# One backward-attention kernel: the dO columns evacuated and summed for four heads at a time instead of two

## The chip, the cores and the metric

The kernel runs on one core of one Trainium2 chip. The metric is the device time of one execution in microseconds (us), as a median over several runs.

## The reference

It computes the forward pass and all gradients of one decode step of a transformer block with conditioning: attention over a cached K and V (2 batches, 32 heads, 8192 positions, 128 wide, bf16), then a gated feed-forward network. Cut to what matters:

```python
q = (h @ wq) per head
scores = einsum('bhqd,bhkd->bhqk', q, k_cache) * Dh ** -0.5
p = softmax(scores); o = einsum('bhqk,bhkd->bhqd', p, v_cache)
x = x + ga * (o @ wo)
...                                   # feed-forward, then jax.vjp of everything
out = (forward, d_x, d_k_cache, d_v_cache, d_wq, d_wo, ...)
```

K and V are 134 MB each. K is read once, V twice (forward and backward), and dK and dV, 134 MB each, are written.

## The kernel before

The program lays all work into numbered slots; within a slot each engine gets its instructions in a fixed order. A head has a forward job A (scores, softmax, o) and a backward job C (dP = dO V, dS, then the outer products dK and dV). In the middle of the run A jobs of batch 1 alternate with C jobs of batch 0; in the last third only C jobs of batch 1 are left.

A C job needs, for its head, the column dO = wo d_attn, that column times the softmax's normaliser (DOr), and SIG, the sum over the width of O times dO. These are made for two heads at a time, in three steps of one slot each:

```python
def steps_do(b, k):
    st = {}
    hs = slice(2 * k, 2 * k + 2)

    def tr():          # 8 transposes of wo blocks, evacuated to kt (DVE in batch 0, ACT in batch 1)
        ...
    def mm():
        ps = scr(2)    # scratch columns in the PSUM tile that the head's scores or dP use as well
        kt = st.pop("kt")
        for n in range(2):
            for dc in range(NC):
                nc.tensor.matmul(ps[:, n:n + 1], kt[:, n * NC + dc, :], d_attn_bf[:, dc, b:b + 1], ...)
        nc.vector.tensor_copy(DO_bf[:, b, hs], ps)
        nc.vector.tensor_mul(DOr_bf[:, b, hs], ps, rtot[:, b, hs])
        pr = tmp.tile([P, 2], F32, name="prod", tag="prod", bufs=2)
        nc.vector.tensor_mul(pr[:], O32[:, b, hs], ps)
        st["pr"] = pr

    def sig():
        ps = scr(2)
        nc.tensor.matmul(ps, onesf[:], st.pop("pr")[:], start=True, stop=True)
        nc.vector.tensor_copy(SIG[:, b, hs], ps)

    return [(1, tr), (1, mm), (1, sig)]
```

`scr` hands out columns 256 and up of the tile `s_ps`, in whose columns 0 to 63 the dP matmuls of the running C job are written. Batch 0's pairs are spread over the run, each a few slots before its heads need it. Batch 1's 16 pairs come one after another, two slots apart, once d_attn of batch 1 is known:

```python
for k in range(H // 2):
    lay(steps_do(0, k), E0 if k == 0 else max(E0 + 3 * k, sC[2 * k] - 10))
...
for k in sorted(range(H // 2), key=lambda k: 2 * k < H - VKEEP):   # the two heads whose V is kept come first
    lay(steps_do(1, k), t1)
    t1 += 2
```

A finished half of dK or dV (1 MB) is stored from its tile, and that tile comes free for the next load only after the store has landed (in the kernel before, the median store landed 12.8 us after its issue; page, part 6):

```python
if o + QK == HK:
    sq_.dma_start(src_of(dst, n)[:, hf * HK:(hf + 1) * HK, :], t[:])   # 1 MB store
    ...                                                             # tile released 6 slots later
```

## Time and profile before

| what | value | view |
|---|---|---|
| time, median of 6 runs | 1748.55 us (1748.49 to 1749.08) | runs |
| span of the profiled run | 1745.8 us | page |
| DMA traffic | 713.55 MB, mean 409 GB/s | page, slices |
| PE, DVE, ACT busy | 79%, 67%, 57% | page, part 1 |
| batch 1's dO stretch | 69.5 us, clock 0.59 | windows |

Batch 1's **stretch** means here the time from the start of the DVE instruction that writes d_attn of batch 1 to the end of the last SIG copy: 1147.92 to 1217.44 us.

From the page of the kernel before: the rows of part 2 cut the span into 40 equal slices; a digit is a share in tenths.

```profile
span 1745.8 us, 54866 instructions
PE 1384.8 (79%) x24113; PEld 1236.8 (71%) x24113; DVE 1170.4 (67%) x1677; ACT 986.7 (57%) x1405; POOL 368.9 (21%) x646
...
PE   6999999989967777777776778788777776785783
...
PEclk9999999988988978888888888775655556566576
DMA  9999999999999999999999999999999999999997
GB/s 381 417 418 417 418 417 390 417 378 415 419 423 410 413 419 419 419 413 415 407 415 411 416 405 398 371 422 423 425 416 420 417 406 397 417 420 411 405 415 315
DMA packets 112955, 713.55 MB, mean 409 GB/s; under 512 B 11303, under 2 KB 20211, under 8 KB 30795
```

The DMA row is full in all slices but the last, and the rate is 405 to 425 GB/s in 33 of the 40 slices. PE is nearly full in the first quarter (412.95 of the first 440 us, by the windows view) and no engine is after that. I read that as a kernel bound by transfers; half_before, sum_x5 and keep0 below test it. The clock row is in tenths of full speed, so 9 is 90% or more and 5 is half.

The waits of the kernel before, whole run. Columns: who waited, for whom, us in total, times, the longest.

```profile
DVE half L1088 <- DMA out_dram<-half: 248.2, 75, 10.6
...
PE s_ps L1065 <- DVE prod L731: 14.2, 22, 1.3
DVE SIG L737 <- PE s_ps L736: 13.9, 16, 1.1
```

The same view of the load queue:

```profile
SPq L177 <- DMA out_dram<-half: 753.0, 92, 18.9
```

Both DVE's outer products (L1088) and the loads (L177) wait most for stores to land.

The windows of the kernel before. Each row: stretch, its length, then busy us (and instructions) of each engine, granted clock, DMA share (1.01 over 0 to 440 and 470 to 1000 us too, where the DMA row is at 9), GB/s.

```profile
core 0: us, PE busy (x) PEld busy (x) DVE busy (x) ACT busy (x) POOL busy (x), PEclk, DMA share, GB/s
1147.92:1217.44 69.52, 59.44 (x815) 56.67 (x813) 50.16 (x115) 41.84 (x53) 8.51 (x16) 0.59 1.01 422
1217.44:1240.00 22.56, 17.10 (x294) 14.95 (x293) 14.39 (x20) 14.81 (x22) 2.35 (x5) 0.76 1.01 425
```

One pair of heads, in order of time. Columns: start, duration, engine, line, operation, output and inputs; in brackets the idle time before it and who ended it.

```profile
1156.36 0.15 DVE L728 CAST DO_bf<-s_ps 128x2 bf16<-128x2 f32 x1
...
1156.49 0.15 DVE L731 TENSOR_TENSOR prod<-O_266,s_ps 128x2 f32<-128x2 f32 x1
...
1156.70 0.34 PE L1065 MATMUL s_ps<-DO_bf,kt 128*128 128x1 bf16 x8 [1.32 <-DVE prod L731]
...
1156.90 0.36 PE L736 MATMUL s_ps<-prod,onesf 128*128 128x2 f32 x2
...
1157.69 0.15 DVE L737 COPY SIG<-s_ps 128x2 f32<-128x2 f32 x1
```

The dP matmuls (L1065) do not use prod, but they write into the PSUM tile that prod still reads, and here PE sat idle for 1.32 us until prod was through. The whole run has 22 such waits, 14.2 us in all.

### The profile page before, as it was taken

The numbers are of one execution on the slowest core, as the hardware profiler recorded it, in microseconds if no ns is written. First come the engines' busy times: TensorE is split into PE (matmuls) and PEld (weight loads), VectorE is DVE, ScalarE is ACT, GpSimd is POOL, SyncE is SP. The second block draws the span as 40 slices with busy tenths as digits, with TensorE's granted clock in tenths as the row PEclk, the third lists the DMA queues.
The fourth block names the chain that finished last, engine by engine and source line by source line (L and its number), as shares of the span: only waits on it lengthen the run. The fifth ranks groups of instructions, "written<-read, shape, count | busy, mean of one in ns | idle before, by whom it ended". The sixth has DMA issues, their size and how long they took to land. (4 is left out here: it accounts for less than half of the span.)

```text
span 1745.8 us, 54866 instructions
## 1 busy us (share of the span) xinstructions
PE 1384.8 (79%) x24113; PEld 1236.8 (71%) x24113; DVE 1170.4 (67%) x1677; ACT 986.7 (57%) x1405; POOL 368.9 (21%) x646
## 2 busy tenths in 40 slices
PE   6999999989967777777776778788777776785783
PEld 5999999979866667677676677778555554574573
DVE  2666666857776676677667668777566666675686
ACT  4666666646544545555454455565656565574683
POOL 0333333312221221222122122111111111110111
PEclk9999999988988978888888888775655556566576
DMA  9999999999999999999999999999999999999997
GB/s 381 417 418 417 418 417 390 417 378 415 419 423 410 413 419 419 419 413 415 407 415 411 416 405 398 371 422 423 425 416 420 417 406 397 417 420 411 405 415 315
DMA packets 112955, 713.55 MB, mean 409 GB/s; under 512 B 11303, under 2 KB 20211, under 8 KB 30795
## 3 DMA queue, kind: packets, MB, share of 16 engines
q1 hardware_dynamic: 70832, 425.81, 60.2%
q0 software_dynamic: 36864, 268.45, 36.9%
q10 hardware_dynamic: 5019, 15.78, 2.3%
q8 instruction: 188, 3.08, 0.7%
q14 instruction: 52, 0.43, 0.1%
HBM read 425.79 MB, written 284.20 MB: 407 GB/s over the span
## 5 line engine op out<-in xcount | busy, mean ns | idle before, releaser
L371 ACT COPY kt<-tp 128x1024 bf16<-128x1024 bf16 x768 | 773.9, 1014 | 574.7 <-PE tp L366 566.4
L366 PE MATMUL tp<-identb,half 128*128 128x128 bf16 x8192 | 778.4, 252 | 13.5 <-DVE kt L369 11.1
L366 PEld LDWEIGHTS <-half 128*128 128x128 bf16 x8192 | 605.3, 113 | 102.8 <-issue 97.5
L1093 POOL DMA_DIRECT2D out_dram<-half x256 | 136.2, 532 | 1036.2 <-DVE half L1088 869.3
L427 PE MATMUL m_ps<-ek,half 128*128 128x129 bf16 x4096 | 325.2, 221 | 0.0
L369 DVE COPY kt<-tp 128x1024 bf16<-128x1024 bf16 x256 | 176.3, 688 | 167.9 <-PE tp L366 166.4
L1065 PE MATMUL s_ps<-DO_bf,kt 128*128 128x1 bf16 x4096 | 192.4, 168 | 114.0 <-DVE kt L369 93.3
L1065 PEld LDWEIGHTS <-kt 128*128 128x128 bf16 x4096 | 188.7, 108 | 129.9 <-DVE kt L369 103.8
L386 PE MATMUL s_ps<-qT_bf,kt 128*128 128x1 bf16 x4096 | 177.6, 164 | 102.6 <-DVE kt L369 100.8
L427 PEld LDWEIGHTS <-half 128*128 128x128 bf16 x4096 | 245.9, 98 | 0.3
L386 PEld LDWEIGHTS <-kt 128*128 128x128 bf16 x4096 | 158.9, 97 | 107.5 <-DVE kt L369 105.0
L1216 ACT CAST stg<-m_ps 128x512 bf16<-128x512 f32 (+2 forms) x124 | 72.2, 582 | 71.0 <-PE m_ps L1215 71.0
L449 PE MATMUL k_ps<-half,pz 128*32 128x512 bf16 x1024 | 68.0, 386 | 21.3 <-POOL pz L435 21.3
L1215 PE MATMUL m_ps<-half 2*128 2x512 bf16 (+2 forms) x124 | 74.1, 598 | 2.1 <-ACT half L1190 1.8
L449 PEld LDWEIGHTS <-pz 128*32 128x32 bf16 x1024 | 21.9, 96 | 41.6 <-POOL pz L435 23.4
L395 PE MATMUL s_ps<-nident,rm 128*128 128x128 bf16 x64 | 15.5, 243 | 22.0 <-DVE rm L390 22.0
L398 DVE TENSOR_REDUCE nm<-s_ps 128x1 f32<-128x128 f32 x64 | 18.6, 290 | 20.3 <-PE s_ps L395 20.3
L1298 ACT COPY kt<-tp 128x1024 bf16<-128x1024 bf16 x28 | 29.0, 1061 | 1.1 <-PE tp L1292 1.0
L712 PE MATMUL tp<-identb,half 128*128 128x128 bf16 x256 | 29.3, 287 | 0.0
L1190 ACT CAST half<-m_ps 2x512 bf16<-2x512 f32 (+1 forms) x36 | 19.9, 564 | 15.8 <-PE m_ps L1187 12.9
L712 PEld LDWEIGHTS <-half 128*128 128x128 bf16 x256 | 24.9, 139 | 0.0
L718 ACT COPY kt<-tp 128x1024 bf16<-128x1024 bf16 x16 | 16.2, 1012 | 14.0 <-PE tp L712 13.5
(871 smaller groups left out, 1766.5 us busy)
## 6 DMA issues: line engine op xcount, KB each, us to landing
out_dram<-half POOLq DMA_DIRECT2D x256, 1024.0 KB, 12.8
half<-in_A_v_cache_dram SPq DMA_DIRECT2D x252, 1024.0 KB, 11.7
half<-in_A_k_cache_dram SPq DMA_DIRECT2D x128, 1024.0 KB, 19.8
out_dram<-stg ACTq DMA_DIRECT2D x22, 512.0 KB, 9.9
half<-in_A_wq_dram SPq DMA_DIRECT2D x8, 1024.0 KB, 10.0
half<-in_B_w_dram SPq DMA_DIRECT2D x6, 1024.0 KB
half<-in_A_wo_dram SPq DMA_DIRECT2D x4, 1024.0 KB, 20.5
half<-in_w_mod_dram SPq DMA_DIRECT2D x3, 1024.0 KB, 16.6
```

Source lines behind the costliest of these rows:

```text
L366: nc.tensor.transpose(tp[:, j, :], block(j), identb[:])
L369: nc.vector.tensor_copy(kt[:], tp[:])
L371: nc.scalar.copy(kt[:], tp[:])
L386: nc.tensor.matmul(S_ps[i][:, cc:cc + 1], kt[:, j, :], qT_bf[:, h, b:b + 1], start=True, stop=True)
L427: nc.tensor.matmul(m[:, 0:P + 1], vb_(i, kk), t[:, kk % QK, 0:P + 1], start=(kk == 0), stop=(kk == KK - 1), skip_group_check=True)
L449: nc.tensor.matmul(kp["ps"][NR * j:NR * (j + 1), :], pz[:, o:o + NR], K[(i, kk // HK)][:, kk % HK:kk % HK + QP, :], start=False, stop=(h = ...
L712: nc.tensor.transpose(tp[:, n * NC + dc, :], wo_of(h, dc), identb[:])
L1065: nc.tensor.matmul(DP[n][:, cc:cc + 1], kt[:, j, :], DO_bf[:, b, h:h + 1], start=True, stop=True)
L1093: sq_.dma_start(src_of(dst, n)[:, hf * HK:(hf + 1) * HK, :], t[:])
L1215: nc.tensor.matmul(ps[:lw, 0:rw], rsl(ln, lc, lw, step), rsl(rn, rc, rw), start=True, stop=True)
L1216: nc.scalar.copy(st["t"][:lw, o:o + rw], ps[:lw, 0:rw])
L1298: nc.scalar.copy(kt[:], tp[:])
```

## The change

Its intent: do these small operations half as often. The transposes and the dO matmuls stay as they are, but two pairs share one scratch block, and one set of evacuations, one ones matmul and one SIG copy. The diff, cut:

```diff
-    def steps_do(b, k):
+    def steps_do(b, k0, k1):
...
-        hs = slice(2 * k, 2 * k + 2)
+        n2 = 2 * (k1 - k0)
+        hs = slice(2 * k0, 2 * k1)
-        def tr():
+        def tr(k):
...
-        def mm():
-            ps = scr(2)
+        def mm(k):
+            if k == k0:
+                st["ps"] = scr(n2)
+            ps = st["ps"]
             kt = st.pop("kt")
             for n in range(2):
+                o = 2 * (k - k0) + n
...                                        # matmuls into column o in place of n
+            if k < k1 - 1:
+                return
             nc.vector.tensor_copy(DO_bf[:, b, hs], ps)
             nc.vector.tensor_mul(DOr_bf[:, b, hs], ps, rtot[:, b, hs])
-            pr = tmp.tile([P, 2], F32, name="prod", tag="prod", bufs=2)
-            nc.vector.tensor_mul(pr[:], O32[:, b, hs], ps)
+            pr = tmp.tile([P, DOG * 2], F32, name="prod", tag="prod", bufs=2)
+            nc.vector.tensor_mul(pr[:, 0:n2], O32[:, b, hs], ps)
...
-        return [(1, tr), (1, mm), (1, sig)]
+        for k in range(k0, k1):
+            out += [(1, lambda k=k: tr(k)), (1, lambda k=k: mm(k))]
+        return out + [(1, sig)]
+
+    DOG = 2
...
-    for k in range(H // 2):
-        lay(steps_do(0, k), E0 if k == 0 else max(E0 + 3 * k, sC[2 * k] - 10))
+    for k in range(0, H // 2, DOG):
+        lay(steps_do(0, k, k + DOG), E0 if k == 0 else max(E0 + 3 * k, sC[2 * k] - 10))
...
-    for k in sorted(range(H // 2), key=lambda k: 2 * k < H - VKEEP):
-        lay(steps_do(1, k), t1)
-        t1 += 2
+    kf = (H - VKEEP) // 2
+    for k0, k1 in [(kf, H // 2), *((k, min(k + DOG, kf)) for k in range(0, kf, DOG))]:
+        lay(steps_do(1, k0, k1), t1)
+        t1 += 2 * (k1 - k0)
```

The number of slots that batch 1's stretch takes is the same.

More of the change, by code (lines that the diff above doesn't have):

```diff
@@ L719, in tr @@
             st["kt"] = kt
-        def mm():
-            ps = scr(2)
+        def mm(k):
+            if k == k0:
+                st["ps"] = scr(n2)
+            ps = st["ps"]
             kt = st.pop("kt")
             for n in range(2):
+                o = 2 * (k - k0) + n
                 for dc in range(NC):
-                    nc.tensor.matmul(ps[:, n:n + 1], kt[:, n * NC + dc, :], d_attn_bf[:, dc, b:b + 1],
+                    nc.tensor.matmul(ps[:, o:o + 1], kt[:, n * NC + dc, :], d_attn_bf[:, dc, b:b + 1],
                                      start=(dc == 0), stop=(dc == NC - 1))
+            if k < k1 - 1:
+                return
             nc.vector.tensor_copy(DO_bf[:, b, hs], ps)
             nc.vector.tensor_mul(DOr_bf[:, b, hs], ps, rtot[:, b, hs])
-            pr = tmp.tile([P, 2], F32, name="prod", tag="prod", bufs=2)
-            nc.vector.tensor_mul(pr[:], O32[:, b, hs], ps)
+            pr = tmp.tile([P, DOG * 2], F32, name="prod", tag="prod", bufs=2)
+            nc.vector.tensor_mul(pr[:, 0:n2], O32[:, b, hs], ps)
             st["pr"] = pr
         def sig():
-            ps = scr(2)
-            nc.tensor.matmul(ps, onesf[:], st.pop("pr")[:], start=True, stop=True)
+            ps = scr(n2)
+            nc.tensor.matmul(ps, onesf[:], st.pop("pr")[:, 0:n2], start=True, stop=True)
             nc.vector.tensor_copy(SIG[:, b, hs], ps)
-        return [(1, tr), (1, mm), (1, sig)]
+        for k in range(k0, k1):
+            out += [(1, lambda k=k: tr(k)), (1, lambda k=k: mm(k))]
+        return out + [(1, sig)]
+    DOG = 2
     def steps_chain(b):
```

## The prediction

> **What bounds the kernel now.** The DMA engines. The page's slices show DMA at 9 (90% or more) in 39 of 40 slices; 713.55 MB move at a mean of 409 GB/s in a span of 1745.8 us. The page's busy shares are lower: PE 79%, DVE 67%, ACT 57%. [...] In the waits of the load queue, loads wait 753.0 us for output stores to drain, by far the longest entry.
>
> **What the change does.** Batch 0's dO pairs are scattered from 448 to 1084 us. All 16 pairs of batch 1, and the last of batch 0, lie between 1146.1 and 1217.5 us. By the instruction order, transposes, their evacuations and the 256 d_attn matmuls stay; groups go from 32 to 17 (8 in batch 0, 9 in batch 1, where the kept pair stays alone and first). Each group has four small DVE operations (DO, DOr, prod, SIG) and one fp32 matmul against ones, recorded as two passes. So 60 DVE instructions of 0.15 to 0.16 us vanish, and 30 PE records of 0.22 to 0.35 us with weight loads of 0.19 to 0.34 us. The rest grow from 2 to 4 columns, which I take to cost nothing visible. No transfer is added, and the load queue's order stays.
>
> **Worth.** DVE: the timeline has three of the four starting 0.07 us apart, so a group takes about 0.4 us: 15 x 0.4 = 6 us, about half of it where batch 1's stretch leaves DVE idle anyway (52 of 71 us busy). PE: at most 15 x 0.6 = 9 us of records. Waits: PE's dP matmuls, whose PSUM tile holds the scratch columns, waited for prod 14.2 us (7.6 in batch 1's stretch); DVE waited 13.9 us for the ones matmul. About half of these should go. If engines bounded batch 1's stretch, it could shorten by 3 to 6 us of 71.
>
> **On the critical path: almost nothing.** In that stretch the windows view gives a DMA share of 1.01 and 423 GB/s, among the best of the run; loads mostly wait for stores (56.1 us), and 14 us for transposes. Engine time gained becomes longer waits for DMA. From 470 to 1000 us the share is 1.01 at 415 GB/s too. The new cost is latency: SIG and DOr of the first four heads come two slots (about 2.5 to 3 us) later, just before head 0's spread; loads in flight should hide it. Buffers freed a little earlier or later may shift the mix of reads and writes, a few us in either direction.
>
> **Prediction: 1748.0 us**, 8 in 10 between 1743.0 and 1752.0. Faster by over 2%: 0.01; within 2%: 0.98; slower by over 2%: 0.01.
>
> **What would show it right.** DO, DOr, prod and SIG at 17 each with unchanged means; DVE busy about 9 us lower by records (60 x 0.15), PE some 8 lower; PE's waits for prod about halved; DMA bytes unchanged, slices still 9; the load queue's waits for stores unchanged or longer; batch 1's stretch within 1 us of 71.4.
>
> **What would make it wrong.** If the stretch from 1146 us shortens by several us and the end moves with it, engines, not DMA, set the pace there. If the later DOr delays the first heads' stores enough to open a gap in DMA near 450 to 470 us, it gets slower. If the last 46 us (DMA share 0.77) change, the tail moved.

## The result, and the profile after

The changed kernel took 1748.24 us (median of 10 runs, 1744.65 to 1750.76), the kernel before 1748.87 us (20 runs, 1747.46 to 1752.12). The ratio is 0.9993, with a 95% interval of 0.9984 to 1.0001: the same.

The page of the changed kernel:

```profile
span 1746.7 us, 54749 instructions
PE 1366.7 (78%) x24083; PEld 1219.9 (70%) x24083; DVE 1165.6 (67%) x1617; ACT 987.1 (57%) x1405; POOL 372.8 (21%) x646
...
PEclk7999999989978888888888888787555556567576
DMA  9999999999999999999999999999999999999997
GB/s 381 417 418 418 418 417 388 418 378 418 419 422 404 412 422 418 413 417 419 415 411 411 407 412 399 381 418 422 427 414 420 419 399 394 416 416 408 405 413 319
DMA packets 112954, 713.54 MB, mean 408 GB/s; under 512 B 11303, under 2 KB 20211, under 8 KB 30795
```

Bytes and DMA row are as before. 60 DVE and 30 PE instructions are gone. But PE's busy time fell by 18.1 us, about twice what those 30 records can account for, and the clock row differs where the stretch lies (slices 27 and 28).

Its waits (L1076 is what L1065 was, L1099 what L1088 was, L737, L742 and L743 what L731, L736 and L737 were):

```profile
DVE half L1099 <- DMA out_dram<-half: 274.2, 75, 19.0
...
PE s_ps L1076 <- DVE prod L737: 2.3, 4, 0.8
...
DVE SIG L743 <- PE s_ps L742: 1.1, 1, 1.1
```

And its load queue:

```profile
SPq L177 <- DMA out_dram<-half: 792.2, 101, 16.8
```

The two waits that the change aims at went from 28.1 to 3.4 us. The waits for stores grew: by 26.0 us on DVE and by 39.2 us for the loads of L177 (27.4 us over all lines of the load queue). Part of that is scatter: in re_before below, the same kernel as before, DVE waited 257.7 us for stores in place of 248.2 and L177 763.9 in place of 753.0. The windows show where the time went:

```profile
core 0: us, PE busy (x) PEld busy (x) DVE busy (x) ACT busy (x) POOL busy (x), PEclk, DMA share, GB/s
1147.18:1201.89 54.71, 45.08 (x797) 42.83 (x795) 47.20 (x83) 41.47 (x53) 8.51 (x16) 0.80 1.01 423
1201.89:1240.00 38.11, 15.64 (x294) 13.88 (x293) 14.26 (x19) 14.41 (x22) 2.13 (x4) 0.65 1.01 424
```

The stretch is 14.8 us shorter (54.7 against 69.5), with the clock at 0.80 against 0.59. But the next row is 15.5 us longer with the same work in it (294 matmuls in both kernels), so by 1240 us the two kernels have done the same matmuls and are level again. The DVE timeline of the changed kernel shows the handover (the `...` stand for lines left out):

```profile
1212.28 1.22 DVE L1099 TENSOR_TENSOR half<-DOr,e_25217 128x2048 bf16<-128x2048 bf16 x1
1232.46 1.22 DVE L1099 TENSOR_TENSOR half<-Qr,ds_25441 128x2048 bf16<-128x2048 bf16 x1 [18.96 <-DMA out_dram<-half]
1237.42 1.23 DVE L1099 TENSOR_TENSOR half<-DOr,e_25533 128x2048 bf16<-128x2048 bf16 x1 [3.74 <-DMA out_dram<-half]
```

The same place in the kernel before:

```profile
1227.02 1.23 DVE L1088 TENSOR_TENSOR half<-Qr,ds_25531 128x2048 bf16<-128x2048 bf16 x1 [3.86 <-DMA out_dram<-half]
...
1232.16 1.22 DVE L1088 TENSOR_TENSOR half<-Qr,ds_25531 128x2048 bf16<-128x2048 bf16 x1
1237.12 1.23 DVE L1088 TENSOR_TENSOR half<-DOr,e_25623 128x2048 bf16<-128x2048 bf16 x1 [3.74 <-DMA out_dram<-half]
```

Counted from the instruction that writes ds, the one at 1232.46 us in the changed kernel is the one at 1232.16 us in the kernel before. The changed kernel reaches this point early, finds no free tile, and waits 18.96 us for a store to land; the kernel before arrives later and does not wait here (it had waited 3.86 us two outer products of dK earlier, at 1227.02). The next instruction starts at 1237.1 and 1237.4 us, set free by a store in both: from there they run alike.

One group of four heads after the change:

```profile
1156.69 0.16 DVE L734 CAST DO_bf<-s_ps 128x4 bf16<-128x4 f32 x1
...
1156.84 0.15 DVE L737 TENSOR_TENSOR prod<-O_266,s_ps 128x4 f32<-128x4 f32 x1
...
1157.04 0.34 PE L1076 MATMUL s_ps<-DO_bf,kt 128*128 128x1 bf16 x8 [0.82 <-DVE prod L737]
...
1157.35 0.34 PE L742 MATMUL s_ps<-prod,onesf 128*128 128x4 f32 x2
...
1158.04 0.16 DVE L743 COPY SIG<-s_ps 128x4 f32<-128x4 f32 x1
```

Four columns cost about what two did: 0.15 to 0.16 us on DVE, and a matmul record of 0.34 us against 0.36.

### The profile page after: what moved, and what is told of

Its sections match the earlier page's. It is cut to its first block, busy times and chain, and to the rows that moved or that the text cites. A ratio compares the mean times of both kernels' runs of the same rounds, so it can differ in the third digit from the quotient of the medians.

```text
span 1746.7 us, 54749 instructions
## 1 busy us (share of the span) xinstructions
PE 1366.7 (78%) x24083; PEld 1219.9 (70%) x24083; DVE 1165.6 (67%) x1617; ACT 987.1 (57%) x1405; POOL 372.8 (21%) x646
## 5 line engine op out<-in xcount | busy, mean ns | idle before, releaser
L371 ACT COPY kt<-tp 128x1024 bf16<-128x1024 bf16 x768 | 774.5, 1014 | 569.5 <-PE tp L366 560.8
L366 PE MATMUL tp<-identb,half 128*128 128x128 bf16 x8192 | 772.1, 250 | 13.6 <-DVE kt L369 10.6
L366 PEld LDWEIGHTS <-half 128*128 128x128 bf16 x8192 | 600.3, 113 | 101.9 <-issue 95.2
L1076 PE MATMUL s_ps<-DO_bf,kt 128*128 128x1 bf16 x4096 | 191.5, 168 | 122.2 <-DVE kt L369 114.3
L1076 PEld LDWEIGHTS <-kt 128*128 128x128 bf16 x4096 | 185.9, 107 | 136.9 <-DVE kt L369 125.0
L427 PEld LDWEIGHTS <-half 128*128 128x128 bf16 x4096 | 247.5, 98 | 0.5 <-issue 0.2
L1201 ACT CAST half<-m_ps 2x512 bf16<-2x512 f32 (+1 forms) x36 | 19.8, 564 | 33.1 <-PE m_ps L1198 30.3
L1309 ACT COPY kt<-tp 128x1024 bf16<-128x1024 bf16 x28 | 29.0, 1060 | 1.1 <-PE tp L1303 1.0
L713 PE MATMUL tp<-identb,half 128*128 128x128 bf16 x256 | 23.4, 246 | 0.0
L488 DVE COPY OK<-m_ps 128x1 f32<-128x1 f32 x64 | 9.9, 154 | 19.2 <-ACT half L487 16.9
L395 PEld LDWEIGHTS <-rm 128*128 128x128 bf16 x64 | 6.3, 98 | 23.2 <-DVE rm L390 23.2
## 6 DMA issues: line engine op xcount, KB each, us to landing
half<-in_A_k_cache_dram SPq DMA_DIRECT2D x128, 1024.0 KB, 19.8
```

The costliest lines, as they stand in the source:

```text
L366: nc.tensor.transpose(tp[:, j, :], block(j), identb[:])
L371: nc.scalar.copy(kt[:], tp[:])
L427: nc.tensor.matmul(m[:, 0:P + 1], vb_(i, kk), t[:, kk % QK, 0:P + 1], start=(kk == 0), stop=(kk == KK - 1), skip_group_check=True)
L713: nc.tensor.transpose(tp[:, n * NC + dc, :], wo_of(h, dc), identb[:])
L1076: nc.tensor.matmul(DP[n][:, cc:cc + 1], kt[:, j, :], DO_bf[:, b, h:h + 1], start=True, stop=True)
L1309: nc.scalar.copy(kt[:], tp[:])
```

## The experiments

My theory: DMA sets the total, the grouping really makes the engines faster in the stretch, and all of that turns into waiting for stores. Rivals: the shorter stretch is luck of the granted clock; or engine time in the stretch is worth nothing even without the DMA bound.

### Both kernels profiled again

No edit. re_before, expected:

> The kernel before, unchanged, profiled a second time. In its first profile batch 1's dO stretch (from the DVE write of d_attn for batch 1 to the end of the last SIG copy) took 69.5 us (1147.9 to 1217.4) at a mean clock near 0.59; in the changed kernel 54.7 us (1147.2 to 1201.9). If the grouping caused the shortening, this repeat is again at 66 to 72 us. If it was luck of the granted clock, this repeat can be anywhere from 52 to 72. Total time within 0.2% in both cases.

Measured: 1749.20 us (one run), stretch 69.3 us, clock 0.57.

re_after, expected:

> The changed kernel, unchanged, profiled a second time. If the grouping caused the shortening: the stretch is again 53 to 58 us, and the engines then stand still for 15 to 25 us waiting for a store to land, just after it. If it was luck of the clock: anywhere from 52 to 72 us. Total time within 0.2% in both cases.

Measured: 1749.62 us (one run), stretch 51.8 us, clock 0.92, then a wait of 20.51 us for a store. The kernel before beside both: 1748.32 us. The stretch kept its length to 0.3 us without the grouping and was 2.9 us shorter still with it (a miss of my 53 to 58). These are two profiles of each kernel; all the profiles below add to them (see the clocks in the section on the prediction). The shortening belongs to the change.

### The change in one batch only

b1_only lays batch 0 in pairs again:

```diff
-    for k in range(0, H // 2, DOG):
-        lay(steps_do(0, k, k + DOG), ...
+    for k in range(0, H // 2):
+        lay(steps_do(0, k, k + 1), ...
```

> Four heads at a time in batch 1 only; batch 0 as before. If the DMA engines set the time and batch 1's grouping is what shortened the stretch: stretch 53 to 58 us, total within 0.2% of before. If the ends of the two kernels differ because of batch 0's later DO, this run sheds it: total 0.05 to 0.1% below before, which three rounds can hardly show.

Measured: 1750.05 us, ratio 1.0006 (0.9990 to 1.0023). Stretch 52.1 us (a little under the 53 expected), clock 0.97, then a wait of 21.21 us for a store.

b0_only lays batch 1 in pairs again:

```diff
-    for k0, k1 in [(kf, H // 2), *((k, min(k + DOG, kf)) for k in range(0, kf, DOG))]:
+    for k0, k1 in [(kf, H // 2), *((k, k + 1) for k in range(kf))]:
```

> Four heads at a time in batch 0 only; batch 1 as before. Expected by the theory: stretch back at 66 to 72 us, the first SIG about 2.5 us later than before, total within 0.2% of before. By the rival (luck of the clock): a stretch anywhere from 52 to 72 us.

Measured: 1749.07 us, ratio 1.0003 (0.9988 to 1.0018). Stretch 67.9 us, clock 0.58. So batch 1's grouping alone shortens the stretch. The later DO and DOr of batch 0 cost nothing that these runs can show.

### Only the evacuations, or only the sums, for four heads

evac4_sum2 keeps the three DVE evacuations at four heads and goes back to one ones matmul and one SIG copy for each pair:

```diff
-        def sig():
-            ps = scr(n2)
-            nc.tensor.matmul(ps, onesf[:], st.pop("pr")[:, 0:n2], start=True, stop=True)
-            nc.vector.tensor_copy(SIG[:, b, hs], ps)
+        def sig(k):
+            o = 2 * (k - k0)
+            ps = scr(2)
+            nc.tensor.matmul(ps, onesf[:], st["pr"][:, o:o + 2], start=True, stop=True)
+            nc.vector.tensor_copy(SIG[:, b, 2 * k:2 * k + 2], ps)
...
-        return out + [(1, sig)]
+        return out + [(1, lambda: [sig(k) for k in range(k0, k1)])]
```

> Only the three DVE evacuations (DO, DOr, prod) are done for four heads at a time; the ones matmul and the SIG copy stay one for each pair, but follow each other in one slot. If the DVE evacuations that PE waits for are what counts: stretch 52 to 58 us. If the halved fp32 ones matmuls count: stretch 62 to 70 us. Total within 0.2%.

Measured: 1747.80 us (one run), stretch 64.6 us, clock 0.58.

evac2_sum4 evacuates each pair at once and sums four heads:

```diff
-            if k < k1 - 1:
-                return
...
+            h2s = slice(2 * k, 2 * k + 2)
+            nc.vector.tensor_copy(DO_bf[:, b, h2s], ps[:, o:o + 2])
...                                        # DOr and prod likewise; sig unchanged
```

> Only the ones matmul and the SIG copy are done for four heads at a time; DO, DOr and prod stay one for each pair. If the DVE evacuations count: stretch 62 to 70 us. If the halved ones matmuls and SIG copies count: 52 to 58 us. Total within 0.2%.

Measured: 1750.73 us (one run), stretch 67.0 us, clock 0.50. I had expected one of the two to carry the gain. Neither did: alone they give 4.9 and 2.5 us against the first profile's 69.5, together 14.8 to 17.7. In these two single profiles the mean clock did not rise (in evac4_sum2 it was full only from about 1190 to 1200 us), so they do not say which part raises it. Nor do they show that it takes both: keep0 below has the full grouping and took 63.5 us, so one profile of each part is too few.

### Stores cut to half their bytes, with and without the change

The outputs dK and dV are wrong on purpose here: only half of each tile is stored, the rest of the outputs is never written. The engines' work is the same; 134 MB of 713.5 are gone.

```diff
-            sq_.dma_start(src_of(dst, n)[:, hf * HK:(hf + 1) * HK, :], t[:])
+            sq_.dma_start(src_of(dst, n)[:, hf * HK:hf * HK + HK // 2, :], t[:, 0:HK // 2, :])
```

> The kernel before with every store of dK and dV cut to half its bytes (the outputs are wrong on purpose): 134 MB fewer of 713.5. If DMA sets the time, the total falls by 150 to 320 us (134 MB at 415 GB/s would be 323, less what the engines then bound). If the engines set it, it falls by less than 30 us. Batch 1's dO stretch stays near 65 to 72 us.

Measured: 1541.43 us (1535.99 to 1546.66), 208 us below the kernel before (1749.43 us beside it), about two thirds of the 323 us that the cut bytes take at 415 GB/s. The kernel is no longer bound by DMA throughout:

```profile
1066.60:1136.10 69.50, 57.62 (x813) 54.94 (x811) 50.23 (x115) 41.95 (x53) 8.53 (x16) 0.61 0.85 305
```

(The stretch of half_before; columns as above.) It takes 69.5 us as ever, but the DMA share in it is 0.85 in place of 1.01.

half_after has the same edit on the changed kernel.

> The changed kernel with the same cut. If the gain of the stretch is real and is lost only because the engines then wait for stores: this run is 8 to 18 us below half_before, and there is no wait of about 19 us for a store after the stretch. If the grouping is worth nothing even without the DMA bound: within 3 us of half_before.

Measured: 1507.12 us (1504.60 to 1510.32), 34.3 us or 2.2% below half_before. That is about twice the most that I had expected. Its stretch, in the windows of half_after:

```profile
1041.50:1093.95 52.45, 40.73 (x790) 38.26 (x789) 46.96 (x83) 41.10 (x52) 8.53 (x16) 0.89 0.96 365
```

The stretch accounts for 17.0 us, and no long wait for a store follows it (the longest until 1160 us is the 2.80 us of this line):

```profile
1116.17 1.23 DVE L1099 TENSOR_TENSOR half<-DOr,e 128x2048 bf16<-128x2048 bf16 x1 [2.80 <-DMA out_dram<-half]
```

More came earlier: d_attn of batch 1 was ready at 1041.5 in place of 1066.6 us, 25.1 us sooner. The two add up to 42 us, of which 36.3 reached the end of the profiled runs (spans of 1541.7 and 1505.4 us); what follows the stretch took 5.8 us longer. The gain before the stretch points at batch 0's groups, so the last run left them out.

half_b1_only: half stores, and four heads at a time in batch 1 only.

> Stores cut to half as in half_before (outputs wrong on purpose), and four heads at a time in batch 1 only. half_after was 34 us below half_before; in the traces 25 us of that had come before d_attn of batch 1 was ready (1041.5 against 1066.6) and 17 us inside batch 1's stretch. If the two parts are separate: d_attn of batch 1 within 4 us of 1066.6, the stretch 50 to 58 us, and a total of 10 to 20 us below half_before (1521 to 1532). If batch 1's grouping alone gives all of it: about 1507.

Measured: 1531.58 us (1527.01 to 1544.18), 9.9 us below half_before by the medians (16.5 by the profiled spans, 1541.7 and 1525.2). Stretch 55.5 us at a clock of 0.78. d_attn of batch 1 came at 1059.3 us, 7 us earlier than in half_before, where I had allowed 4; batch 0's program is the same in both, so 7 us is also what these times scatter by. With less DMA in the way, batch 0's grouping is worth some 20 to 24 us (by the spans and by the medians, 1531.58 less 1507.12), and that is clear of the spread. Batch 1's share would be about 10 to 17 us, but its runs spread over 17 us, one of them (1544.18) lies above half_before's median, and they ran on another chip. So the shorter stretch shows in the traces (14.0 us here, 17.0 in half_after), while batch 1's share of the total is not shown by itself.

What fits batch 0's share are the waits before batch 1's stretch. Those of half_before, over 450 to 1066 us:

```profile
DVE SIG L737 <- PE s_ps L736: 15.1, 12, 1.7
...
PE s_ps L1065 <- DVE prod L731: 5.0, 10, 0.5
```

and of half_after over the same time:

```profile
DVE SIG L743 <- PE s_ps L742: 1.1, 1, 1.1
...
PE s_ps L1076 <- DVE prod L737: 0.8, 2, 0.4
```

In half_b1_only, where batch 0 is in pairs again, the wait for the ones matmul is back at 15.7 us and that for prod at 7.0. In the instruction order of the kernel before, the SIG copy of 12 of batch 0's 16 pairs stands directly behind prod on DVE, so DVE stands still while PE works its way to the ones matmul: 12 waits. With the longer groups the steps fall into other slots, and in seven of the eight groups two or more other DVE operations stand between prod and SIG. That fits an effect of place, not of count: nearly the whole wait went, not half. No run moved SIG alone, so it is argued. These waits fell by 18.2 us, beside the 20 to 24 us of batch 0's share; no run shows that each of them counted in full.

### The other direction: more engine time in the stretch

sum_x5 is the kernel before with batch 1's ones matmul issued five times (same result):

```diff
-            nc.tensor.matmul(ps, onesf[:], st.pop("pr")[:], start=True, stop=True)
+            pr = st.pop("pr")
+            for _ in range(5 if b == 1 else 1):
+                nc.tensor.matmul(ps, onesf[:], pr[:], start=True, stop=True)
```

> The kernel before with each of batch 1's 16 ones matmuls issued five times in place of once (same result): 64 more fp32 matmuls of two passes, recorded at about 0.55 us each when the clock is low, so the stretch grows by 20 to 35 us, from 69 to about 90 to 105. If DMA has slack for that: total within 3 us of before. If the backlog of transfers that hides the stretch runs out: the DMA share falls below 0.97 in the stretch and the total rises by 5 to 25 us.

Measured: 1766.37 us, ratio 1.0099 (1.0080 to 1.0119), 18.4 us above the kernel before beside it. Stretch 96.6 us. Its windows:

```profile
1150.00:1170.00 20.00, 17.18 (x185) 16.66 (x183) 10.44 (x26) 8.90 (x12) 1.60 (x3) 0.55 0.95 367
1170.00:1190.00 20.00, 18.03 (x199) 17.37 (x198) 11.09 (x26) 8.33 (x9) 1.59 (x3) 0.50 0.85 321
1190.00:1210.00 20.00, 18.14 (x193) 17.57 (x191) 10.48 (x22) 8.64 (x12) 2.13 (x4) 0.50 0.76 283
1210.00:1230.00 20.00, 18.49 (x209) 18.00 (x210) 9.86 (x23) 9.45 (x12) 1.59 (x3) 0.57 0.69 255
```

The DMA share sinks step by step. Of 27.1 us more, 18.4 reach the end. The stretch was thus near balance in the kernel before: made 15 us shorter it gives nothing, made 27 us longer it costs most of it.

### Bytes

keep0 is the changed kernel without the two V heads of batch 1 that stay on chip between forward and backward: four more loads of 1 MB.

```diff
-    VKEEP = 2
+    VKEEP = 0
...                                        # and no separate first group in batch 1
```

> The changed kernel, but no V head of batch 1 is kept on chip: four more loads of 1 MB. If bytes set the time: 4.19 MB at about 415 GB/s, so 10 us more than before (8 to 13). If the engines set it: within 3 us.

Measured: 1759.09 us, ratio 1.0058 (1.0043 to 1.0073), 11.2 us more than the kernel before by the medians. 4.19 MB at the page's mean of 408 GB/s are 10.3 us. Bytes count in full, where 15 us of engine time in the stretch counted for nothing. By the way, this run's stretch was 63.5 us with the grouping, at a clock of 0.63: the gain of the stretch is not always the same.

The opposite, four kept heads, did not build: the tiles ran out.

### Eight heads at a time

Eight heads in both batches was refused by the simulator: a C job of batch 0 would read DOr before it is written (this too is not in the record). So eight_b1 does it in batch 1 only:

```diff
-    DOG = 2
+    DOG = 4                                # batch 0 keeps groups of two pairs
```

> Batch 1 in groups of eight heads (four pairs), batch 0 in groups of four: the cost that was cut is cut again. By the theory the stretch is 48 to 54 us, the wait for a store after it 20 us or more, and the total within 0.2% of before. If engine time in the stretch counted for the total, it would be 2 to 5 us below before.

Measured: 1747.55 us, ratio 0.9995 (0.9980 to 1.0011). Stretch 50.5 us at a clock of 0.91, as expected; of the waits for stores after it the longest is 17.7 us, not 20, and 4.89 us follow. No version that I tried beats the two kernels.

## Why the prediction was right or wrong

**The total: right, and for the stated reason.** "Engine time gained becomes longer waits for DMA." The stretch became 14.8 us shorter and the engines then waited 18.96 us for one store; at 1237 us both kernels were level. Half stores show that the grouping's engine time counts where DMA leaves room (34.3 us, both batches together), keep0 that bytes count in full (11.2 us more for 4.19 MB, which take 10.3 us at the page's mean rate). That the number itself came within 0.3 us (1748.0 against 1748.24) is luck: the runs of the changed kernel spread over 6.1 us.

**The counts: right.** DO, DOr, prod and SIG at 17 each, with unchanged means of 0.15 to 0.16 us. Added up by records the four fell from 19.8 to 10.5 us on DVE (9 were forecast) and the ones matmuls from 13.9 to 6.5 us on PE (8 were forecast). The bytes are unchanged and the load queue's waits for stores longer (753.0 to 792.2 us).

**The stretch "within 1 us of 71.4": wrong.** (The prediction counts from 1146.1 us, so its 71.4 is the 69.5 of this document.) The step that failed is "Engine time gained becomes longer waits for DMA" applied within the stretch: the waits came after it. A DMA share of 1.01 says that transfers were queued throughout. It does not say that engines waited for them there. In that stretch of the kernel before no DVE operation waited for a store; the engines set its length, and the queue had enough in it to stay full.

**"If engines bounded batch 1's stretch, it could shorten by 3 to 6 us": mis-sized.** It was 14.8 us, 17.7 in the repeat. I counted records and waits at a fixed clock. From one DO cast to the next but one, two unchanged pairs of batch 1 took 8.1 to 8.9 us in the kernel before, and 8.7 to 8.9 where the clock was at half; with the grouping, four heads took 6.0 to 6.3 us in the changed kernel while the clock was full, and 7.7 (changed kernel) to 8.4 us (keep0) when it was at half. So at half clock the grouping saves some 0.3 to 1.2 us for four heads; most of the rest goes with the clock. No two unchanged pairs ran at full clock throughout, so what the grouping saves there is not shown. The mean clock in the stretch was 0.50 to 0.61 in all seven profiles without the full grouping in batch 1, and 0.80, 0.92, 0.97, 0.91, 0.63, 0.89 and 0.78 in the seven with it. So the shorter stretch goes with the change, by way of the clock; what in the change lifts the clock is not settled.

**"About half of these should go": mis-sized.** Of 28.1 us of waits on prod and on the ones matmul 3.4 were left. In batch 0 the wait for the ones matmul fell from 13.1 to 1.1 us, which fits the better place of the SIG copy in DVE's order, and the dP matmuls' wait on prod from 6.6 us to none; in batch 1's stretch the wait on prod fell from 7.6 to 2.3. Why the waits on prod fell by more than half was not taken apart.

**"DVE busy about 9 us lower", "PE some 8 lower": right by records, not by the page.** The page's DVE busy time fell by 4.8 us, since it counts overlapping records once (three of the four start 0.07 us apart; the prediction's own 15 x 0.4 = 6 us allowed for that). PE's fell by 18.1 us, 15.8 of them from the start of the stretch to 1240 us, where its granted clock was 0.74 in place of 0.63.

**The later first DOr: right.** Nothing opened in DMA between 440 and 470 us (417 GB/s and a share of 1.01 in both), and b0_only is the same as before.

## What to carry to other kernels

Where DMA is full from end to end, as it is here, expect an engine-side saving to be worth only what it frees in transfers (here 14.8 us less in the stretch left the total at a ratio of 0.9993, and 4.19 MB more cost 11.2 us). Look for the wait that grows right after the stretch that shrank, and test the saving's real size by cutting bytes, even with wrong outputs. A full DMA share does not prove that the engines of that stretch are waiting (in the kernel before the share was 1.01 and no DVE operation there waited for a store): the queue may be living on its backlog (in sum_x5 the share sank from 0.95 to 0.69), and then engine time is free in one direction only (here 15 us less gave nothing and 27 us more cost 18.4).

## What the traces show besides

- In the changed kernel PE was busy 15.54 of 16 us (1184 to 1200 us) and the granted clock stayed at 0.50; in the repeat of the same kernel, in the same window, PE was busy 11.59 of 16 us at 1.00. The trace models the ends of matmuls, so its busy time is rough. Read as it stands, a PE busy throughout did not bring the full clock in these 16 us; what sets the clock no run shows. The windows of the changed kernel, then of its repeat:

```profile
1184.00:1188.00 4.00, 3.88 (x60) 3.80 (x61) 3.79 (x6) 2.62 (x3) 0.53 (x1) 0.50 1.01 414
...
1196.00:1200.00 4.00, 3.88 (x53) 3.76 (x52) 2.39 (x4) 2.56 (x5) 0.53 (x1) 0.50 1.00 418
```

```profile
1184.00:1188.00 4.00, 2.66 (x65) 2.49 (x62) 3.56 (x4) 3.03 (x4) 1.06 (x2) 1.00 1.02 424
...
1196.00:1200.00 4.00, 2.71 (x55) 2.38 (x52) 3.49 (x10) 2.32 (x5) 1.06 (x2) 1.00 1.02 422
```

- Loads and stores of 1 MB tiles, mixed, moved 422 to 426 GB/s in the kernel before from 1145 to 1218 us (windows of 15 to 20 us).
- The DO casts took 150 to 165 ns with 2 columns in the kernel before, and 152 to 164 ns in the changed kernel, 15 of 17 with 4 columns: twice the columns cost nothing that these records show.
